# A chunked-attention and gated-MLP kernel: the first weight block is queued behind two inputs, and the second unit's scores and softmax are written ahead of the first unit's values

## The chip, the cores and the metric

The kernel runs on one core of one Trainium2 chip. The metric is the device time of one execution in microseconds. The five engines run side by side, each taking its own instructions in order: TensorE (PE: matmuls and transposes), VectorE (DVE), ScalarE (ACT), GpSimd (POOL) and SyncE (SP, which here issues nearly all transfers). They wait for each other through semaphores.

## The reference

What must be computed, cut to its core (the inputs q and k are drawn with a standard deviation of about 0.4, v with 0.1):

```python
# q, k, v: (8, 8, 576, 64); attention inside chunks of 64 tokens
scores = q_c @ k_c.T / 8;  scores -= max(scores)
attn = exp(scores);  attn /= sum(attn) + 1e-9
out = attn @ v_c
x = out, heads side by side             # (4608, 512)
xn = x / sqrt(mean(x*x) + 1e-6) * rms_g
g = xn @ w_gate                         # (512, 1536)
result = (g * sigmoid(g) * (xn @ w_val)) @ w_out
```

## The kernel before, in words

The 4608 tokens are cut into 18 units of 256 tokens. A unit has two subtiles of 128 tokens, numbered through, so unit 0 is subtiles 0 and 1, and unit 1 is subtiles 2 and 3. The MLP works on tiles of 512 tokens, two units each, and its 1536 hidden columns go in twelve blocks f of 128. The first three MLP tiles are processed one at a time, the rest in pairs. This case is about the stretch before the first MLP matmul and the first two blocks f of the first tile.

**Numbers in two parts.** The matmuls of the MLP run in a rounded 32-bit type, so every operand is split into a high part and a remainder, and each product is three matmuls (high by high, high by low, low by high). A weight block therefore has to be converted before it is used. `conv_load(n)` loads block n (1 MB, tile `raw`) on SP's queue. `conv_start(n)` makes two ACT passes over it (L178, an absolute value into tile `w`, and L179, in place). `conv_join(n)` has three DVE passes (L187, L188, L191) and an ACT cast that writes the high part (L204), and for the gate and value blocks also stores `w` to DRAM. `conv_end(n)` is a DVE subtraction that writes the low part (L212). Block 0 and block 1 are the gate and value weights of f = 0 and f = 1; block 2 is the output weights of both. I call them weights 0, 1 and 2.

**The start of the program** (the plain list of calls from L1091 on):

- `load_first_unit` loads q and k of unit 0 in two halves into the space of `x`, q on SP's queue and k on ACT's. `load_first_values` loads v of unit 0 (512 KB), `load_unit(1)` q, k and v of unit 1 (`qt`, `kt`, `vt`, 512 KB each).
- For each subtile: `scores` (32 small matmuls, L266), `softmax` (DVE maximum and subtraction, ACT exponential L283; for unit 1 both subtiles at once in `softmax_both`, L566, L568, L572), `att_transpose` (4 PE transposes of the exponentials, L324, copied out by ACT, L325), `softmax_sum` (DVE), `att_values` (32 small matmuls with v, L446), and `first_norm` (DVE, L532, which writes `x`).
- Then the RMS norm of a unit: `first_squares` (ACT, L544, which writes its unneeded squares into the subtile's old exponential tile `e`), `first_root` (ACT L145 and a power on POOL, L146), `first_scale` (ACT, L552 and L556, in place on `x`).
- Then `x` is turned by PE (`x_turn_unit`, L506), and written as high parts by ACT (L512, tile `xh`) and low parts by DVE (L518, tile `xl`). With these the first MLP matmuls start (L587). Their two results `ps_g` and `ps_v` lie in the two buffers of one pool; a silu on ACT (L605) reads `ps_g` and sets that buffer free for the next block f.

The tile pool for `e` has two buffers, so the exponentials of subtile 2 go where those of subtile 0 were, and must wait until `first_squares` has used that space.

**What sets the order.** A scheduler places the instructions of each engine, going by its own estimates of time, from the calls in program order; what results is one fixed list for each engine. Only PE's order from the second MLP tile on is held to program order, and all engines' in the down-projection of the pairs. SP's queue is such a list too, and a transfer waits there until the one eight places before it has landed.

Of the kernel before, what the change touches and what calls it, by code (L numbers as in the profile page):

```python
# [80 lines left out]
def tile_chunk_attn_swiglu(  # L81
# [47 lines left out]
    def bank(pool, name):  # L129
        return pool.tile([P, 512], F32, tag=pool_tag[id(pool)], name=name)  # L130
# [36 lines left out]
    def conv_load(n):  # L167
        if n < len(pairs):
            kind, f = pairs[n]
            nc.sync.dma_start(raws[n], w_up[f] if kind == "up" else w_out[f // 2])  # L170
# [56 lines left out]

    state = {}

    def load_unit(u):  # L230
        qt = io.tile([P, NPAIR, UT], F32, tag="io", name="qt")
        kt = io.tile([P, NPAIR, UT], F32, tag="io", name="kt")
        vt = io.tile([P, NPAIR, UT // CH, D], F32, tag="io", name="vt")
        nc.sync.dma_start(qt, qT[u])
        nc.sync.dma_start(kt, kT[u])
        nc.sync.dma_start(vt, v[u])
        for s in range(2):
            state[2 * u + s] = {"q": qt, "k": kt, "v": vt}

    def load_first_unit():  # L240

        qt, kt = (x[:, 2 * i : 2 * i + 2].rearrange("p s (a t) -> p (s a) t", t=UT) for i in range(2))
        for s in range(2):
            part = slice(s * P, (s + 1) * P)
            nc.sync.dma_start(qt[:, :, part], qT[0][:, :, part])
            nc.scalar.dma_start(kt[:, :, part], kT[0][:, :, part])
            state[s] = {"q": qt, "k": kt}

    def load_first_values():
        vt = io.tile([P, NPAIR, UT // CH, D], F32, tag="io", name="vt")  # L250
        nc.sync.dma_start(vt, v[0])
        for s in range(2):
            state[s]["v"] = vt

    def two_banks(pool, name):
        return [bank(pool, f"{name}{j}").rearrange("p (s c) -> p s c", s=2) for j in range(2)]

    def scores(i, banks):
        st, s = state[i], i % 2
        st["s"] = [b[:, s].rearrange("p (a k) -> p a k", k=CH) for b in banks]  # L260
        for pr in range(NPAIR):
            for j in range(2):
                for c in range(2):
                    tok = s * P + c * CH
                    rows = slice(j * D, (j + 1) * D)
                    nc.tensor.matmul(  # L266
                        st["s"][j][c * CH : (c + 1) * CH, pr],
                        st["q"][rows, pr, tok : tok + CH],
                        st["k"][rows, pr, tok : tok + CH],
                        start=True,  # L270
                        stop=True,
                    )
# [12 lines left out]
    def softmax_sum(i):  # L285
        st = state[i]
        rs = st["rs"] = small.tile([P, NPAIR, 2, 1], F32, name="rs")
        nc.vector.tensor_reduce(rs, st["e"], axis=AX.X, op=ALU.add)
        nc.vector.tensor_scalar_add(rs, rs, 1e-9)
        nc.vector.reciprocal(rs, rs)  # L290
# [27 lines left out]
    def att_transpose(i, pool=None):  # L318
        st = state[i]
        e = st["e"].rearrange("p a j k -> p a (j k)")  # L320
        eT = st["eT"] = att.tile([P, NPAIR, P], F32, tag="eT", name="eT")
        pt = bank(pool or ps_a, "ps_t").rearrange("p (a k) -> p a k", k=P)
        for pr in range(NPAIR):
            nc.tensor.transpose(pt[:, pr], e[:, pr], ident)  # L324
        nc.scalar.copy(eT, pt)  # L325
# [112 lines left out]
    def att_values(i, banks):  # L438
        st, s = state[i], i % 2
        eT, vt = st["eT"], st["v"]  # L440
        st["o"] = [b[:, s].rearrange("p (a d) -> p a d", d=D) for b in banks]
        for pr in range(NPAIR):
            for j in range(2):
                for c in range(2):
                    rows = slice(j * CH, (j + 1) * CH)
                    nc.tensor.matmul(  # L446
                        st["o"][j][c * CH : (c + 1) * CH, pr, :],
                        eT[rows, pr, c * CH : (c + 1) * CH],
                        vt[rows, pr, 2 * s + c, :],
                        start=True,  # L450
                        stop=True,
                    )
# [74 lines left out]
    def first_norm(i):  # L527
        st = state[i]
        xs = x[:, i]
        xv = xs.rearrange("p (j b a d) -> p j a b d", j=2, b=2, d=Q)  # L530
        for j in range(2):
            nc.vector.tensor_tensor(  # L532
                xv[:, j],
                st["o"][j].rearrange("p a (b d) -> p a b d", b=2),
                st["rs"][:, :, j].rearrange("p a (o i) -> p a o i", i=1).broadcast_to([P, NPAIR, 2, Q]),
                op=ALU.mult,
            )

    def first_squares(u):
        ss = state["ss", u] = small.tile([P, 2], F32, name="ss_u")  # L540
        for s in range(2):
            st = state.pop(2 * u + s)
            spent = st["e"].rearrange("p a j k -> p (a j k)")
            nc.scalar.activation(spent, x[:, 2 * u + s], AF.Square, accum_out=ss[:, s : s + 1])  # L544
# [13 lines left out]
    def softmax_both(u, banks):  # L558
        both = [state[2 * u + s] for s in range(2)]
        es = [att.tile([P, NPAIR, 2, CH], F32, name="e") for _ in both]  # L560
        mx = small.tile([P, 2, 2, NPAIR, 1], F32, name="mx_u")
        for st, e in zip(both, es):
            st["e"] = e
        for j in range(2):
            by_row = banks[j].rearrange("p s (a k) -> p s a k", k=CH)
            nc.vector.tensor_reduce(mx[:, j], by_row, axis=AX.X, op=ALU.max)  # L566
            for s, (st, e) in enumerate(zip(both, es)):
                nc.vector.tensor_tensor(  # L568
                    e[:, :, j], st["s"][j], mx[:, j, s].broadcast_to([P, NPAIR, CH]), op=ALU.subtract
                )  # L570
        for e in es:
            nc.scalar.activation(e, e, AF.Exp, scale=SCALE)  # L572
# [465 lines left out]
    def unit_steps(u, x):  # L1038
# [26 lines left out]
        def sixth():  # L1065
            for i in both:
                turned_scale(i)

        return [
            lambda: load_unit(u),  # L1070
            first,
            second,
# [16 lines left out]
            self.n += 1  # L1089

    load_first_unit()  # L1091
    conv_load(0)
    load_first_values()
    load_unit(1)
    nc.sync.dma_start(g_col, rms_g)
    for n in range(1, AHEAD):
        conv_load(n)
    s0, s1, s2 = (two_banks(p, "ps_s") for p in (ps_a, ps_h, ps_acc))
# [5 lines left out]
    softmax_sum(0)  # L1104
    att_transpose(1)
    softmax_sum(1)
    o = two_banks(ps_h, "ps_o")
    att_values(0, o)
    first_norm(0)
    o = two_banks(ps_acc, "ps_o")  # L1110
    att_values(1, o)
    first_norm(1)
    scores(2, s2)
    scores(3, s2)
    softmax_both(1, s2)
    first_squares(0)
    first_root(0)
    first_scale(0, False)
# [24 lines left out]
    for t in range(PLAIN):  # L1143
# [39 lines left out]
        for f in range(NF):  # L1183
            g = gated(f, CONVS[f % 2], conv_step)
            if t == 0:
                if f in (0, 5):
                    u = 2 + (f == 5)
                    load_unit(u)
                    sc = two_banks(ps_a, "ps_s")
                    for i in (2 * u, 2 * u + 1):  # L1190
                        scores(i, sc)
                    if f:
                        softmax_rows(u, sc)
                    else:
                        softmax_whole(u, sc)
                elif f in (2, 7):
                    for i in (2 * u, 2 * u + 1):
                        att_transpose(i)
                elif f in (3, 8):
                    o = two_banks(ps_a, "ps_o")  # L1200
                    for i in (2 * u, 2 * u + 1):
                        att_values(i, o)
                    norm_unit(u, o)
                if f == NF - 1:
                    x_transpose((0, 1))
            elif t == 1 and f == NF - 1:
                for dt in range(NDT):
                    x_split(dt, blocks(x)[:, :, dt], slice(0, TT))
# [18 lines left out]
    for b in range(NB):  # L1227
# [3 lines left out]
        if b + 1 < NB:  # L1231
            u = 2 * t + 4
# [82 lines left out]
```

## Time and profile before

| | |
|---|---|
| median of 3 runs | 905.02 us (904.91 to 908.19) |
| the profiled execution | 905.95 us, its span 904.2 us |
| PE busy in the span | 881.3 us (97%) |
| DVE, ACT, POOL busy | 610.7, 482.1, 191.7 us |
| first MLP matmul (L587) starts | 31.23 us |
| granted TensorE clock | 1.00 throughout |

The span is the time between the first and the last recorded instruction; 1.75 us of the profiled execution lie around it. All stage times in this document are microseconds from the start of the span. In a row of the timeline the first number is the start, the second the duration; a bracket at its end tells how long the engine was idle before it, and what ended that. In a row of transfers the last number is the time from issue to landing.

### The profile page before, as it was taken

What the parts mean: (1) busy time and instruction counts of PE and PEld (TensorE: products, weight loads), DVE (VectorE), ACT (ScalarE), POOL (GpSimd) and SP (SyncE); (2) the same over time, 40 slices, a digit from 0 to 9 for tenths busy, and PEclk for the clock granted to TensorE, in tenths of its full rate; (3) what the DMA queues carried; (4) which work ended last, traced back from release to release, by engine and by line L of the source; (5) the groups of instructions that cost most, each with busy time, mean ns of one, the idle gap of its engine ahead of it and who ended that gap; (6) DMA issues with size and microseconds to landing.
All of it is one profiled execution on the core that took longest, in us unless ns stands there. A gap on an engine that the chain in (4) does not pass through costs nothing. (4 is left out here: it accounts for less than half of the span.)

```text
span 904.2 us, 17484 instructions
## 1 busy us (share of the span) xinstructions
PE 881.3 (97%) x6828; PEld 721.2 (80%) x6828; DVE 610.7 (68%) x984; ACT 482.1 (53%) x795; POOL 191.7 (21%) x163
## 2 busy tenths in 40 slices
PE   4899999999999999999999999999999999999998
PEld 3688888888888888887888878887878788888886
DVE  6999865464567755885577997645768953334776
ACT  5998934353457665565556644545647522222452
POOL 0004040342200000233323012332330114323201
PEclk9999999999999999999999999999999999999999
DMA  9799999787987864698887777776876784445342
GB/s 350 280 336 337 329 333 344 247 259 234 296 267 217 260 201 168 256 292 290 308 264 296 316 258 256 273 264 203 302 246 240 275 340 185 158 149 207 165 163 94
DMA packets 85795, 231.85 MB, mean 256 GB/s; under 512 B 8912, under 2 KB 45264, under 8 KB 71504
## 3 DMA queue, kind: packets, MB, share of 16 engines
q1 hardware_dynamic: 84656, 230.20, 72.7%
q8 instruction: 54, 0.88, 0.4%
q10 hardware_dynamic: 1056, 0.52, 0.2%
q14 instruction: 29, 0.24, 0.1%
HBM read 167.25 MB, written 63.44 MB: 255 GB/s over the span
## 5 line engine op out<-in xcount | busy, mean ns | idle before, releaser
L815 PE MATMUL ps_c<-xp,wr 128*128 128x512 f32 x432 | 104.6, 391 | 0.0
L815 PE MATMUL ps_b<-xp,wr 128*128 128x512 f32 x432 | 104.5, 391 | 0.0
L815 PE MATMUL ps_a<-xp,wr 128*128 128x512 f32 x432 | 104.3, 390 | 0.0
L587 PE MATMUL ps_g<-xh,parts 128*128 128x512 f32 x288 | 96.7, 396 | 0.9 <-ACT xh L512 0.6
L587 PE MATMUL ps_v<-xh,parts 128*128 128x512 f32 x288 | 94.9, 390 | 0.0
L815 PEld LDWEIGHTS ps_a<-xp,wr 128*128 128x128 f32 x432 | 80.9, 188 | 17.3 <-DMA wr<-wsd 0.3
L815 PEld LDWEIGHTS ps_b<-xp,wr 128*128 128x128 f32 x432 | 80.7, 188 | 17.0
L815 PEld LDWEIGHTS ps_c<-xp,wr 128*128 128x128 f32 x432 | 80.6, 188 | 17.0
L622 PE MATMUL acc<-parts,gh 128*128 128x512 f32 x288 | 90.0, 394 | 0.0
L587 PEld LDWEIGHTS ps_g<-xh,parts 128*128 128x128 f32 x288 | 54.5, 189 | 13.5 <-ACT xh L512 1.0
L935 ACT CAST gh<-g 128x512 fp32r<-128x512 f32 x72 | 43.6, 621 | 37.3 <-PE ps_c L1024 13.2
L587 PEld LDWEIGHTS ps_v<-xh,parts 128*128 128x128 f32 x288 | 54.2, 188 | 11.2
L903 POOL TENSOR_TENSOR g<-u,u 128x512 f32<-128x512 f32 x18 | 23.2, 1288 | 186.9 <-ACT u L871 70.6
L622 PEld LDWEIGHTS acc<-parts,gh 128*128 128x128 f32 x288 | 53.2, 188 | 11.2
L940 DVE TENSOR_TENSOR gl<-g,gh 128x512 fp32r<-128x512 f32 x72 | 49.3, 695 | 13.1 <-PE ps_c L1024 4.0
L587 PE MATMUL ps_g<-xl,parts 128*128 128x512 f32 x144 | 56.6, 393 | 0.0
L609 DVE TENSOR_TENSOR sg<-ps_v,sg 128x512 f32<-128x512 f32 x36 | 24.7, 686 | 47.0 <-PE ps_v L587 30.4
L622 PE MATMUL acc<-parts,gl 128*128 128x512 f32 x144 | 56.2, 391 | 0.0
L587 PE MATMUL ps_v<-xl,parts 128*128 128x512 f32 x144 | 56.0, 389 | 0.0
L893 POOL TENSOR_TENSOR p<-p,p 128x512 f32<-128x512 f32 x36 | 46.7, 1310 | 33.5 <-DVE p L892 31.8
L815 PE MATMUL ps_d<-xp,wr 128*128 128x512 f32 x216 | 52.3, 391 | 0.0
L871 ACT ACTIVATE p<-p 128x512 f32<-128x512 f32 x36 | 22.6, 632 | 54.4 <-POOL p L893 52.0
(150 smaller groups left out, 1747.4 us busy)
## 6 DMA issues: line engine op xcount, KB each, us to landing
wr<-wsd SPq DMA_DIRECT2D x63, 1024.0 KB, 7.3
wo<-osd SPq DMA_DIRECT2D x30, 1024.0 KB, 7.9
raw<-w_up_dram SPq DMA_DIRECT2D x12, 1024.0 KB, 10.5
vt<-v_dram SPq DMA_DIRECT2D x18, 512.0 KB, 5.3
wsd<-parts SPq DMA_DIRECT2D x18, 512.0 KB, 8.3
qt<-qT_dram SPq DMA_DIRECT2D x17, 512.0 KB, 5.6
kt<-kT_dram SPq DMA_DIRECT2D x17, 512.0 KB, 6.3
away_e<-e SPq DMA_DIRECT2D x28, 256.0 KB, 3.0
```

Of the source, the lines that this page charges most:

```text
L587: nc.tensor.matmul(ps, a[f][:, cols], b[dt], start=(dt == 0 and i == 0), stop=(dt == NDT - 1 and i == 2),)
L609: nc.vector.tensor_tensor(sg, pv, sg, op=ALU.mult)
L622: nc.tensor.matmul(acc[s], a[:, cols], b, start=(f == 0 and i == 0), stop=(f == NF - 1 and i == 2),)
L815: nc.tensor.matmul(ps, w[:, a, m, cols], xp[:, b, kt], start=start and kt == 0 and i == 0, stop=stop and kt == 1 and i == 2, skip_group_ch ...
L871: nc.scalar.activation(t, t if src is None else src, AF.Silu)
L893: nc.gpsimd.tensor_tensor(kp["p5"], kp["p1"], kp["p5"], op=add)
L903: nc.gpsimd.tensor_tensor(g[:, 0, 1], kp["u2"], kept[0]["u2"], op=mult)
L935: nc.scalar.copy(gh, src)
L940: nc.vector.tensor_tensor(gl, src, pair[0].bitcast(F32), op=ALU.subtract)
```

## The change

Two things are written in another order; no instruction is added or removed.

1. The load of weights 0 leaves its place right behind q and k of unit 0, and is issued behind v of unit 0 and q and k of unit 1, ahead of v of unit 1.
2. `scores(2)`, `scores(3)` and `softmax_both(1)` are called ahead of `att_values` and `first_norm` of unit 0.

```diff
-    def load_unit(u):
+    def load_unit(u, then=None):
         ...
         nc.sync.dma_start(qt, qT[u])
         nc.sync.dma_start(kt, kT[u])
+        if then is not None:
+            then()
         nc.sync.dma_start(vt, v[u])
@@
     load_first_unit()
-    conv_load(0)
     load_first_values()
-    load_unit(1)
+    load_unit(1, lambda: conv_load(0))
@@
     softmax_sum(1)
+    scores(2, s2)
+    scores(3, s2)
+    softmax_both(1, s2)
     o = two_banks(ps_h, "ps_o")
     att_values(0, o)
     first_norm(0)
     o = two_banks(ps_acc, "ps_o")
     att_values(1, o)
     first_norm(1)
-    scores(2, s2)
-    scores(3, s2)
-    softmax_both(1, s2)
```

The lists of the engines differ in more places than that, since the scheduler works from the new order. PE's list is the same again from the early part of the second MLP tile on. Lines of the changed kernel have numbers that are higher by 2. Three places matter.

**First, PE, from the transposes of subtile 0 to the values of unit 0** (`ps_t` takes the transposes, `ps_o` the values, `ps_s` the scores, `kt,qt` are k and q of unit 1). Before:

```order
L324 MATMUL ps_t<-ident,e 128x128 x8
L446 MATMUL ps_o_263<-vt,eT 64x64 x2
...
L446 MATMUL ps_o_284<-vt,eT 64x64 x2
L266 MATMUL ps_s_193<-kt,qt 64x64 x2
...
L266 MATMUL ps_s_194<-kt,qt 64x64 x2
L324 MATMUL ps_t<-ident,e 128x128 x8
```

Now:

```order
L326 MATMUL ps_t<-ident,e 128x128 x4
L268 MATMUL ps_s_193<-kt,qt 64x64
L326 MATMUL ps_t<-ident,e 128x128 x4
L268 MATMUL ps_s_193<-kt,qt 64x64
L268 MATMUL ps_s_194<-kt,qt 64x64 x2
...
L448 MATMUL ps_o_306<-vt,eT 64x64 x2
...
L326 MATMUL ps_t<-ident,e 128x128 x4
```

All 64 score matmuls of unit 1 now stand ahead of the 64 value matmuls of unit 0, and the first of them stands ahead of the transposes of subtile 1.

**Second, DVE and ACT, from the softmax of unit 0 to that of unit 1** (`mx_u` and `e` are the maxima and exponentials of unit 1, `w` and `raw` a weight block in conversion). DVE before:

```order
L187 TENSOR_SCALAR w<-w 128x1024
L532 TENSOR_TENSOR x<-ps_o_263,rs 128x4x2x32
...
L188 SCALAR_TENSOR_TENSOR w<-w,raw 128x1024
L532 TENSOR_TENSOR x<-ps_o_283,rs 128x4x2x32
...
L191 SCALAR_TENSOR_TENSOR w<-raw,w 128x1024
L566 TENSOR_REDUCE mx_u<-ps_s_193 128x8
```

DVE now:

```order
L568 TENSOR_REDUCE mx_u<-ps_s_193 128x8
L568 TENSOR_REDUCE mx_u<-ps_s_194 128x8
L534 TENSOR_TENSOR x<-ps_o_306,rs 128x4x2x32
...
L187 TENSOR_SCALAR w<-w 128x1024
L534 TENSOR_TENSOR x<-ps_o_326,rs 128x4x2x32
...
L570 TENSOR_TENSOR e<-ps_s_193,mx_u 128x4x64
L570 TENSOR_TENSOR e<-ps_s_194,mx_u 128x4x64
L188 SCALAR_TENSOR_TENSOR w<-w,raw 128x1024
```

ACT now, in the same stretch:

```order
L327 COPY eT<-ps_t 128x512 x2
L178 ACTIVATE w<-raw 128x1024
L179 ACTIVATE raw<-raw 128x1024
L546 ACTIVATE e,ss_u<-x 128x512 x2
L145 ACTIVATE ss_u<-ss_u 128x2
L574 ACTIVATE e<-e 128x512
L554 ACTIVATE x<-x,ri_u 128x512
L558 ACTIVATE x<-x,ri_u 128x512
L327 COPY eT<-ps_t 128x512
L574 ACTIVATE e<-e 128x512
L178 ACTIVATE w<-raw 128x1024
L327 COPY eT<-ps_t 128x512
```

On DVE the maxima of unit 1 moved ahead of both norms of unit 0, and the last pass over weights 0 (L191) behind the exponentials' subtraction. On ACT the two exponentials of unit 1 are now apart, each ahead of the first pass over weights 1 (before, both stood right behind it); the two passes over weights 0 still stand ahead of the squares of unit 0.

**Third, ACT, from the high parts of `x` of unit 1 to the first silu.** Before:

```order
L512 ACTIVATE xh_121<-ps_x,g_col 128x256
L512 ACTIVATE xh_122<-ps_x,g_col 128x256
L179 ACTIVATE raw<-raw 128x1024
L204 CAST parts<-w 128x1024
L178 ACTIVATE w<-raw 128x1024
L605 ACT_TABLE_LOAD
L605 ACTIVATE sg<-ps_g 128x512
```

Now, from a little earlier on:

```order
L558 ACTIVATE x<-x,ri_u 128x512
L204 CAST parts<-w 128x1024
L514 ACTIVATE xh_119<-ps_x,g_col 128x256
...
L514 ACTIVATE xh_122<-ps_x,g_col 128x256
L204 CAST parts<-w 128x1024
L178 ACTIVATE w<-raw 128x1024
L179 ACTIVATE raw<-raw 128x1024 x2
L607 ACT_TABLE_LOAD
L607 ACTIVATE sg<-ps_g 128x512
```

The cast of weights 0 (the first L204 here) moved from well ahead of the norm of unit 1 to right behind it, and between the last high part and the table load there is now one pass over a weight block more than before.

## The prediction

> **What bounds the kernel now.** I read the stages first (windows: stretch, then busy time and instruction count of PE, its weight loads, DVE, ACT, POOL, then granted clock, DMA share, GB/s), then PE's waits.
>
> ```profile
> 0.00:31.00 31.00, 15.94 (x284) 12.71 (x284) 21.64 (x47) 20.14 (x35) 2.13 (x9) 1.00 0.95 368
> 31.00:140.00 109.00, 108.43 (x721) 89.21 (x722) 93.32 (x120) 85.18 (x135) 21.45 (x10) 1.00 0.90 318
> 140.00:240.00 100.00, 100.00 (x800) 82.25 (x800) 49.66 (x86) 42.47 (x74) 29.46 (x24) 1.00 0.85 270
> ```
>
> From 31 us on PE has no idle time worth naming: 0.57 us in 109, then none in 100. Only the first 31 us, where it idles for 15.06, can give anything. The waits of PE there (total, times, longest):
>
> ```profile
> PE ps_s L266 <- DMA x<-qT_dram: 5.7, 2, 5.1
> PE ps_t L324 <- ACT e L572: 4.5, 1, 4.5
> PE ps_x L506 <- ACT x L552: 2.2, 1, 2.2
> PE ps_g L587 <- ACT sg L605: 0.3, 1, 0.3
> ```
>
> The 5.7 us is the first load and isn't touched. The 4.5 us is unit 1's transposes waiting for its exponentials; the change is at that place. The timeline around it, rows picked and put by engine:
>
> ```profile
> 6.81 1.13 PE L266 MATMUL ps_s<-x 64*64 64x64 f32 x32 [0.59 <-DMA x<-qT_dram]
> 10.10 1.12 PE L324 MATMUL ps_t<-ident,e 128*128 128x128 f32 x4 [0.60 <-ACT e L283]
> 11.60 1.98 PE L446 MATMUL ps_o<-vt,eT 64*64 64x64 f32 x64 [0.39 <-ACT eT L325]
> 13.88 1.98 PE L266 MATMUL ps_s<-kt,qt 64*64 64x64 f32 x64 [0.29 <-DMA kt<-kT_dram]
> 20.39 1.97 PE L324 MATMUL ps_t<-ident,e 128*128 128x128 f32 x8 [4.53 <-ACT e L572]
> 11.12 0.69 DVE L187 TENSOR_SCALAR w<-w 128x1024 f32<-128x1024 f32 x1
> 13.44 1.22 DVE L188 SCALAR_TENSOR_TENSOR w<-w,raw 128x1024 int32<-128x1024 int32 x1
> 14.57 0.75 DVE L532 TENSOR_TENSOR x<-ps_o,rs 128x256 f32<-128x256 f32 x2
> 16.37 1.28 DVE L566 TENSOR_REDUCE mx_u<-ps_s 128x8 f32<-128x512 f32 x2
> 17.57 1.41 DVE L568 TENSOR_TENSOR e<-ps_s,mx_u 128x256 f32<-128x256 f32 x4
> 9.95 1.13 ACT L178 ACTIVATE w<-raw 128x1024 f32<-128x1024 f32 x1
> 11.93 1.15 ACT L179 ACTIVATE raw<-raw 128x1024 int32<-128x1024 uint32 x1
> 15.41 0.63 ACT L544 ACTIVATE e<-x 128x512 f32<-128x512 f32 x1 [1.09 <-DVE x L532]
> 16.52 0.71 POOL L146 TENSOR_TENSOR ri_u<-ss_u,mhalf 128x2 f32<-128x2 f32 x1 [15.23 <-ACT ss_u L145]
> 17.89 0.70 ACT L556 ACTIVATE x<-x,ri_u 128x512 f32<-128x512 f32 x1
> 18.70 1.12 ACT L178 ACTIVATE w<-raw 128x1024 f32<-128x1024 f32 x1
> 19.72 1.14 ACT L572 ACTIVATE e<-e 128x512 f32<-128x512 f32 x2
> ```
>
> Unit 1's scores end at 15.86, yet its exponentials start only at 19.72. Its subtraction (17.57) needs the maxima and unit 0's squares (which use the old buffer of `e`); the exponentials then stood behind the scaling of unit 0 and L178 on weights 1. So the 4.5 us is ACT's and DVE's queue, not late scores.
>
> **The change part by part.** First the transfers (of each its issue in the timeline, then its row in the view of transfers):
>
> ```profile
> 2.35 0.62 SPq L170 DMA_DIRECT2D raw<-w_up_dram  x1
> raw<-w_up_dram SPq DMA_DIRECT2D x1, 1024.0 KB, 7.5
> 3.97 0.43 SPq L235 DMA_DIRECT2D kt<-kT_dram  x1
> kt<-kT_dram SPq DMA_DIRECT2D x1, 512.0 KB, 9.8
> ```
>
> Weights 0 landed at 9.85, `kt` at 13.77. Behind the weights came three blocks of 512 KB (v of unit 0, `qt`, `kt`) in 3.92 us, 1.31 each; the first transfers end at 6.81, where PE's wait ends. Moved ahead of the weights, `kt` lands at 6.81 + 3.92 = 10.73 at the earliest. The 1 MB of weights 0 took 3.04 after 6.81 where two blocks at 1.31 take 2.62, so 0.42 of start-up may be added: 11.15. I take 10.9. **Weights 0 land at 13.8**, in `kt`'s old place, since the same bytes are ahead of them: 3.9 later. No transfer is added, and the ones behind land as before; the weights hold up no later load.
>
> PE. The first score matmul of unit 1 stands ahead of subtile 1's transposes and waits for `kt`: the transposes start at 11.0 (before 10.10), end at 12.0; the 64 scores (1.98) end at 14.0, 1.9 earlier than before; the 64 value matmuls (1.98) end at 16.0, 2.4 later.
>
> DVE. It has nothing to do until the scores end: maxima 14.0 + 1.3 = 15.3, first norm (0.7 to 0.75 a subtile) 16.0, L187 on weights 0 (0.69; its ACT pass ended at 13.8 + 1.1 = 14.9) 16.6, second norm 17.3 where it was 15.32. This is the price of moving the values back: +2.0 on unit 0's norm.
>
> ACT (whose next instruction overlaps the one before by about 0.1: 18.70 + 1.12 is past the next start, 19.72, by that). L178 and L179 on weights 0 fill 13.8 to 16.0. The squares of subtile 1 follow the second norm and end with their read-out at 18.1, the small scale at 18.3; the first exponential of unit 1 (0.63) stands next, **18.3 instead of 19.72**; POOL's power (0.71) ends at 19.0; the two scalings, which ended at 18.59, end at 20.4. Then the copy of subtile 2's transposes (0.6), the second exponential (ends 21.4), L178 on weights 1 (1.04 until the next can start), and the copy of subtile 3 (PE's transposes took 1.1 and end at 22.5) at 22.6. That was at 23.31: 0.7 is left of the 1.4 gained. The rest of the way, rows picked from the timeline:
>
> ```profile
> 23.31 0.59 ACT L325 COPY eT<-ps_t 128x512 f32<-128x512 f32 x1
> 23.78 1.07 ACT L204 CAST parts<-w 128x1024 fp32r<-128x1024 f32 x1
> 26.99 0.47 ACT L512 ACTIVATE xh<-ps_x,g_col 128x256 fp32r<-128x256 f32 x1
> 27.35 0.21 ACT L145 ACTIVATE ss_u<-ss_u 128x2 f32<-128x2 f32 x1
> 29.00 0.71 ACT L556 ACTIVATE x<-x,ri_u 128x512 f32<-128x512 f32 x1
> 31.23 0.80 PE L587 MATMUL ps_g<-xh,parts 128*128 128x512 f32 x1 [0.56 <-ACT xh L512]
> 37.30 1.28 ACT L605 ACT_TABLE_LOAD   x1
> 38.52 0.39 PE L587 MATMUL ps_v<-xh,parts 128*128 128x512 f32 x1
> 38.60 0.60 ACT L605 ACTIVATE sg<-ps_g 128x512 f32<-128x512 f32 x1
> 39.25 0.50 PE L587 MATMUL ps_g<-xh,parts 128*128 128x512 f32 x1 [0.34 <-ACT sg L605]
> 44.82 0.61 PE L622 MATMUL acc<-parts,gh 128*128 128x512 f32 x2
> 47.63 1.16 PE L266 MATMUL ps_s<-kt,qt 64*64 64x64 f32 x64
> ```
>
> From 22.6 on ACT is the queue that matters: copy (0.5), L179 on weights 1 (1.05), two high parts of unit 0 (0.9), L178 on weights 2 (1.05) bring it to 26.5. Two squares (1.2), a high part, the small scale at 28.1 (before 27.35); then POOL's 0.71 and the scalings, done at 30.4 (before 29.71): +0.7. L191 on weights 0, which DVE now does only near 20 to 21.5, lets the cast (L204) come late; ACT has it right here, 30.4 to 31.4. Only then come unit 1's first two high parts, and **the first MLP matmul at 32.3, +1.1**. But the four transposes that stood behind the first two matmuls are done by then, so the 24 matmuls of f = 0 end where they ended: the last starts near 38.5.
>
> The first silu is next. After the last high part at 34.15 ACT has L204 (0.95), L178 (1.04), two L179 (1.06 each) and the table load (1.28): the silu starts at 39.5 where it was 38.60, ends at 40.1, and frees `ps_g` for f = 1, which starts at 40.1 and not 39.25: **+0.9**. From there PE is the bound again if the weights keep ahead. DVE is then behind by an L187 and an L188 (0.69 + 1.22) and by the 0.9 itself, but the low part of the output weights of f = 0 is written by 43.1 in this walk, and PE asks for them 5.57 after f = 1 starts (44.82 - 39.25), at 45.7. I add nothing; with that cover gone, it would cost what is missing of these 2.6.
>
> Sum: 0.9 on the profiled 905.95, or 906.8; that execution lay 0.93 above the median of 905.02, so the prediction for the median is **905.9 us**. Bounds: were ACT never to wait from 13.8 on, its work up to the silu (23.1 us: the rows of its list from L178 on weights 0 to the table load, by these durations) would end at 36.9, 1.7 ahead of before; and the landing's +-0.3 and ACT's small waits give +-1.3 on the other side.
>
> [...] The granted clock reads 1.00 everywhere, but the same 64 score matmuls took 1.98 us at 13.88 and 1.16 at 47.63, so the trace agrees with two rates. [...] I keep the sum at the slow durations.
>
> **The rivals.** *A: the earlier exponential carries through.* For it: 4.53 is the longest wait after the first load, and the exponential does move forward by 1.4. If ACT's waits closed up on the way (1.7 above), PE would start f = 1 about 1.5 earlier: 903.5. The whole 4.53 would give 900.5. Against it: unit 0's norm, 2.0 later, feeds the scalings on the same engine. *B, the slower side: the late weights at the head of ACT's queue.* L178 on weights 0 waits for its transfer ahead of the squares; what stands behind is late once that pass starts after 14.6, for its two passes and the first squares (2.1 + 0.6) then run past 17.3, where the second norm ends. If the 3.92 passed down the list whole, 905.0 + 3.9 = 908.9. For it: both engines go in order, and DVE's L187 stands ahead of the second norm. Against it: until 16.0 DVE has no norm ready either, so most of the 3.9 lies under the scores and maxima of unit 1. *C: nothing moves at the end*: the high parts run a little earlier, the silu's delay is taken up in front of f = 1, and it is 905.0.
>
> **How the numbers follow.** My forecast 0.62 (its own range 904.6 to 907.2), A 0.18 (0.03 of it for the whole gap), B 0.10, C 0.10. The range goes down to 903.3, which takes in most of A and the gap-free ACT, and up to 908.0, which leaves out the heart of B: about 0.82. A measurement of this kernel can tell about 0.5%, 4.5 us, from no change. Faster than 900.5 is only A whole, 0.03; slower than 909.5 is B with something on top, 0.04; 0.93 is left for the same.
>
> **What would show it.** Unit 1's scores ending near 14, the values near 16; L178 on weights 0 starting at 13.8; unit 1's first exponential near 18.3; the wait of its transposes down from 4.5 to about 2.9; the last scaling near 30.4; the first MLP matmul near 32.3, and f = 1 near 40.1 behind a wait for the silu of about 1 us. PE idling anywhere later, for weights, would break the step where I added nothing; a first MLP matmul ahead of 31 would be A, one behind 34 B.

## The result, and the profile after

The changed kernel takes 913.55 us (median of 6 runs, 912.45 to 914.91), the kernel before 905.4 beside it (904.69 to 908.19): a ratio of 1.0075, 95% interval 1.0059 to 1.009. It is **slower by about 7 us** (6.8 by the ratio; the two medians lie 8.2 apart) where 905.9 was forecast and 908.0 was the upper end of the range. The profiled execution took 912.45 us with a span of 910.7; before it was 905.95 and 904.2. The stages of the changed kernel (columns as in the prediction):

```profile
0.00:31.00 31.00, 14.79 (x280) 11.77 (x280) 18.29 (x44) 17.27 (x31) 2.65 (x9) 0.81 0.86 322
31.00:140.00 109.00, 104.42 (x688) 84.30 (x689) 92.69 (x116) 87.67 (x135) 21.14 (x10) 0.98 0.89 313
140.00:240.00 100.00, 100.00 (x808) 82.46 (x807) 51.62 (x88) 43.92 (x75) 26.36 (x23) 1.00 0.83 271
```

The clock of 0.81 in the first stage isn't itself a loss: the reading falls to 0.50 from about 19 to 36 us, but the first MLP matmul takes 0.80 us there, as it did in the kernel before at a reading of 1.00.

PE is as full as before from 140 us on. But between 31 and 140 it has 4.6 us of idle time where it had 0.6. PE's waits in the changed kernel:

```profile
PE ps_t L326 <- ACT e L574: 3.6, 1, 3.6
PE ps_x L508 <- ACT x L554: 3.1, 1, 3.1
PE ps_t L326 <- ACT e L308: 2.6, 1, 2.6
PE ps_s L268 <- DMA kt<-kT_dram: 1.7, 1, 1.7
PE ps_g L589 <- ACT sg L607: 1.5, 2, 1.0
PE ps_o L448 <- ACT eT L327: 1.5, 1, 1.5
```

Four rows are of the start, and the row of `ps_g` is so in part: 1.0 of it is the wait of f = 1, 0.51 a wait at 96.19. The third is new and lies elsewhere: L308 is the exponential of `softmax_rows`, the softmax of unit 3, a hundred microseconds into the program. To see where the time went I paired the MLP matmuls (L587 before) of two kernels by rank and subtracted their starts. The "lag" of the changed kernel, at these times of the kernel before:

| before, us | 31.2 | 39.6 | 75.6 | 93.2 | 104.1 | 111.7 | 298.0 |
|---|---|---|---|---|---|---|---|
| lag, us | +2.20 | +2.27 | +2.32 | +2.99 | +6.05 | +6.55 | +6.56 |

So there are **two losses: 2.3 us at the start, and 4.2 between 85 and 112 us**. At the end of the span 6.5 is left of both.

**The start.** Rows of the changed kernel's timeline, picked and put by engine:

```profile
7.78 1.13 PE L268 MATMUL ps_s<-x 64*64 64x64 f32 x32 [1.54 <-DMA x<-qT_dram]
11.61 0.44 PE L268 MATMUL ps_s<-kt,qt 64*64 64x64 f32 x2 [1.65 <-DMA kt<-kT_dram]
14.70 1.55 PE L448 MATMUL ps_o<-vt,eT 64*64 64x64 f32 x63
33.42 0.80 PE L589 MATMUL ps_g<-xh,parts 128*128 128x512 f32 x1
41.52 0.50 PE L589 MATMUL ps_g<-xh,parts 128*128 128x512 f32 x1 [1.00 <-ACT sg L607]
17.49 0.75 DVE L534 TENSOR_TENSOR x<-ps_o,rs 128x256 f32<-128x256 f32 x2
18.82 1.22 DVE L188 SCALAR_TENSOR_TENSOR w<-w,raw 128x1024 int32<-128x1024 int32 x1
19.95 0.75 DVE L570 TENSOR_TENSOR e<-ps_s,mx_u 128x256 f32<-128x256 f32 x2
19.44 1.16 POOL L146 TENSOR_TENSOR ri_u<-ss_u,mhalf 128x2 f32<-128x2 f32 x1 [18.15 <-ACT ss_u L145]
13.98 1.14 ACT L178 ACTIVATE w<-raw 128x1024 f32<-128x1024 f32 x1 [0.27 <-DMA raw<-w_up_dram]
19.20 0.61 ACT L574 ACTIVATE e<-e 128x512 f32<-128x512 f32 x1
21.26 0.70 ACT L558 ACTIVATE x<-x,ri_u 128x512 f32<-128x512 f32 x1
31.19 0.71 ACT L558 ACTIVATE x<-x,ri_u 128x512 f32<-128x512 f32 x1
40.87 0.60 ACT L607 ACTIVATE sg<-ps_g 128x512 f32<-128x512 f32 x1
```

The second half of unit 0's q arrived at 7.78 in this execution and not at 6.81. That comes and goes: 6.81 and 7.02 in two of the runs below with the same start, 7.58 in one with the start of before. The lag at f = 1 of the first two is +2.05 and +2.09, so it isn't the cause.

**Unit 3.** ACT's timeline in the kernel before, the ends of the pieces:

```profile
87.35 1.28 ACT L306 ACT_TABLE_LOAD   x1 [0.44 <-DVE mx_u L301]
88.65 0.31 ACT L306 ACTIVATE e<-ps_s,mx_u 128x64 f32<-128x64 f32 x1
...
91.25 0.60 ACT L605 ACTIVATE sg<-ps_g 128x512 f32<-128x512 f32 x1
91.87 1.28 ACT L306 ACT_TABLE_LOAD   x1
...
98.30 1.28 ACT L605 ACT_TABLE_LOAD   x1
99.59 0.60 ACT L605 ACTIVATE sg<-ps_g 128x512 f32<-128x512 f32 x1
```

and in the changed kernel:

```profile
92.53 1.28 ACT L308 ACT_TABLE_LOAD   x1 [0.75 <-DVE mx_u L303]
93.82 0.31 ACT L308 ACTIVATE e<-ps_s,mx_u 128x64 f32<-128x64 f32 x1
94.25 1.28 ACT L607 ACT_TABLE_LOAD   x1
95.54 0.60 ACT L607 ACTIVATE sg<-ps_g 128x512 f32<-128x512 f32 x1
96.15 1.28 ACT L308 ACT_TABLE_LOAD   x1
...
102.23 1.28 ACT L607 ACT_TABLE_LOAD   x1
103.52 0.60 ACT L607 ACTIVATE sg<-ps_g 128x512 f32<-128x512 f32 x1
104.14 1.28 ACT L308 ACT_TABLE_LOAD   x1
105.43 0.31 ACT L308 ACTIVATE e<-ps_s,mx_u 128x64 f32<-128x64 f32 x1
```

In these rows each change between exponential and silu brings a table load of 1.28 us on ACT. Before, the sixteen exponentials stood in two pieces, 4 | 12, all ahead of the second silu shown (the eighth of the program). Now they stand as 1 | 14 | 1: one piece more, and the last exponential alone behind that silu and two table loads. PE needs all sixteen for its transposes:

```profile
96.19 0.50 PE L589 MATMUL ps_g<-xh,parts 128*128 128x512 f32 x1 [0.51 <-ACT sg L607]
101.77 0.60 PE L326 MATMUL ps_t<-ident,e 128*128 128x128 f32 x4
105.89 0.66 PE L326 MATMUL ps_t<-ident,e 128*128 128x128 f32 x4 [2.59 <-ACT e L308]
```

In the kernel before no wait stands at this place. The lists of ACT and DVE are made anew for the whole program from the new order of the calls, so an edit at 10 us can place an exponential at 105 us.

### The profile page after: what moved, and what is told of

It reads as the page before. It is cut to its first block, busy times and chain, and to the rows that moved or that the text cites. A ratio compares the mean times of both kernels' runs of the same rounds, so it can differ in the third digit from the quotient of the medians.

```text
span 910.7 us, 17495 instructions
## 1 busy us (share of the span) xinstructions
PE 882.3 (97%) x6828; PEld 720.7 (79%) x6828; DVE 611.4 (67%) x984; ACT 485.4 (53%) x797; POOL 192.1 (21%) x163
## 4 chain that ended last, share of the span: by engine, by line
PE 85%; DMA 5%; DVE 5%; ACT 3%; issue 1%; SPq 1%; POOL 0%; DVEq 0%; POOLq 0%; ACTq 0%
PE ps_c L817 11%; PE ps_b L817 11%; PE ps_a L817 11%; PE acc L624 9%; PE ps_g L589 8%; PE ps_v L589 8%; PE ps_d L817 5%; PE ps_c L1026 5%; PE ps_a L1026 5%; PE ps_b L1026 5%; PE ps_d L1026 2%; PE ps_o L390 2%; PE ps_s L268 2%; DMA wr<-wsd 2%; DMA kt<-kT_dram 1%
```

## The experiments

Each kernel ran beside the kernel before on its chip; ratios are to that. Line numbers shift by up to 6 with the edits. The theories: **L**, the start's loss is the late weights; **O**, it is the reordering; **S**, unit 3's loss is how the list places exponentials among silus; **B**, unit 3 is late because the start is. P, Q, S2 and W come up later and are told where they are tested.

**The two parts alone.** One kernel has only the calls reordered, one only the load moved.

```diff
 # e1_scores_only: after, without
-    load_unit(1, lambda: conv_load(0))
+    conv_load(0)    # behind load_first_unit, as before
+    load_unit(1)
 # e2_load_only: after, with scores(2), scores(3), softmax_both(1) behind first_norm(1) again
```

> Second half of the change alone: scores and softmax of unit 1 ahead of unit 0's values, the load of weights 0 in its old place. Theory L (the late weights cost the start of the MLP): weights 0 land near 9.9 again, and f = 1 starts within 0.7 us of the kernel before (39.25). Theory O (moving the values behind the scores costs it): f = 1 starts 1.5 us or more late, near 41. Both then see the list of ACT near 90 us: unit 3's sixteen exponentials stand in three pieces (1, 13, 2) with silus between. Theory S (the piece behind the second silu stalls PE by about 2.6 to 3.2 us, at the transposes of unit 3): a wait of PE for the exponentials of 2.5 or more, total 909 to 912. Theory B (that wait is only the conversion's backlog on DVE): no such wait where the weights come early, total 905 to 907.

> First half of the change alone: weights 0 loaded behind v of unit 0 and q and k of unit 1, program order of scores and values as before. Theory L: weights 0 land near 13.8, their first ACT pass starts there, f = 1 starts 2 us or more late (41.3). Theory O: f = 1 within 0.7 us of 39.25. The exponentials of unit 3 are in three pieces here too (1, 11, 4): theory S: a wait of 2.6 to 3.5 at unit 3's transposes, so 910 to 913 with L's delay and 908 to 910 with O's; theory B: the wait is there only with L's delay.

Reordering alone: 910.51 (ratio 1.0046, 1.0028 to 1.0063), a lag of +1.2 at f = 1 and +3.65 at 104 us. Load alone: 911.55 (1.0054, 1.0033 to 1.0074), -0.16 at f = 1, then +3.54 at 104 and +4.14 at 112. L falls: late weights alone cost the start nothing. The reordering costs it 1.2, less than O's 1.5, and 2.1 to 2.4 with the late load under it. And B is in trouble, for the load's kernel isn't late at 85 us, yet loses 4.3 there. Its exponentials ran as 1 | 11 | 4, those of the other as 1 | 12 | 3 (not 13 and 2). S's sizes missed too: PE's waits for the last piece were 1.73 in the load's kernel and 2.08 in the other, shorter than S allowed, and the load's 911.55 lies above S's 910 (beside a kernel before at 907.18 here). The load's kernel waits another 0.93 for the silu behind the first piece.

**The last piece brought forward, and its control.** Unit 3's exponentials get a higher priority, in the changed kernel and in the one before.

```diff
+            with tc.high_priority(offset=250):
                 for j in range(2):
                     for pr in range(NPAIR):
                         nc.scalar.activation(e[:, pr, j], ...)   # softmax_rows
```

> The changed kernel with a higher priority for unit 3's exponentials: ACT's list is the changed kernel's up to there, then all exponentials stand ahead of the second silu (pieces of 1 and 15 and no third one behind it). Theory S (the one exponential behind a silu and two table loads is the 2.6 us wait, and with it the loss of 4.2 us from 93 to 108 us): the wait falls under 0.6, the lag behind the kernel before stays at +2.3 to +3.2 past 110 us, total about 910 (913.5 less 3.5). Theory B (DVE's maxima, 5.2 us late, are what is late, however the exponentials are cut): PE waits as long at another place there, total 912.5 to 914.5.

> Control: the same priority on the kernel before, whose exponentials already stand in two pieces (4 and 12) ahead of the second silu and stay so. Both theories: 905.4 +- 1, no wait of PE at unit 3's transposes.

The changed kernel now has 1 | 15 and takes 910.1 (1.0035, 1.0023 to 1.0048); the lag is +2.05 at f = 1 and +3.92 at 112 us, 2.6 less than without. In the kernel before the list stays 4 | 12, and the time 906.65 (0.9998, 0.9984 to 1.0011). Between 85 and 112 us 1.8 were still lost, more than S allowed (a lag of at most +3.2): PE waits 0.51 for the silu behind the first piece, 0.22 for the last exponentials and 0.23 for a weight block's low part, and the first matmuls behind such a wait start 0.34 us apart for 0.23.

**All sixteen in one piece, ahead of a silu.** The offset is 300.

> The changed kernel with the sixteen exponentials of unit 3 marked urgent, so that they stand in ScalarE's list in one piece behind five silus: two table loads there instead of five, nothing left behind a later silu. Theory S (the way the list cuts the exponentials costs the second half of the loss): PE's lag behind the kernel before is +2.0 to +2.3 us at f=1 and still at most +2.5 at 112 us; the time is 2 to 2.5 us above the kernel before. Rival B (the work is late because the start is late): the lag grows to about +4 by 112 us, as in the run with two pieces, and the time is 3.5 to 4.5 us above.

914.81 (1.0087, 1.007 to 1.0103): S's numbers missed, and B's too. The piece now stands ahead of the seventh silu of the program (the text above counts one too few), and pulls PE's transposes forward with it. That silu starts at 100.03, behind 4.7 us of exponentials and two table loads; PE waits three times:

```profile
96.70 1.22 PE L327 MATMUL ps_t<-ident,e 128*128 128x128 f32 x4 [0.92 <-ACT e L309]
98.77 1.11 PE L327 MATMUL ps_t<-ident,e 128*128 128x128 f32 x4 [0.86 <-ACT e L309]
100.68 0.79 PE L590 MATMUL ps_g<-xh,parts 128*128 128x512 f32 x1 [0.79 <-ACT sg L608]
```

By the third, PE's granted clock is down as well (0.50 in this stage):

```profile
100.00:104.00 4.00, 3.32 (x8) 2.64 (x9) 3.10 (x4) 3.99 (x6) 0.00 (x0) 0.50 0.93 255
```

Of the 6.6 us lost there, 2.6 are these three waits; about 2 are ten MLP matmuls at the lower clock, 0.43 from start to start where 0.23 is usual. So few table loads aren't enough: what counts is what stands ahead of the silu, or of the transpose, that PE reaches next. This became theory S2.

**The same cut put into the kernel before.** Its start is untouched; the last exponential gets a lower priority, which gives 4 | 11 | 1.

```diff
+                    with order_of(s * 2 * NPAIR + j * NPAIR + pr):   # 15: offset -90
                         nc.scalar.activation(e[:, pr, j], ...)
```

> The kernel before with the last of unit 3's sixteen exponentials given a lower priority, so that they stand in three pieces, 4 | 11 | 1, the last alone behind one more silu and two more table loads; the start is untouched. Theory S: no lag until 90 us, then PE waits 1.5 to 2.6 us on that exponential and the lag stays: 2 to 4 us slower than before. Rival B: without a late start the cut is covered by the MLP's matmuls, and the time is within 0.5 us of before.

911.5 (1.0048, 1.003 to 1.0066). The lag is +0.27 at 93 us, +4.83 at 104, +5.34 at 112. **This cut costs the old kernel 5 us**, with no change at the start; S had allowed at most 4. B falls: a late start isn't needed. The wait, and the stages behind it:

```profile
105.22 0.66 PE L330 MATMUL ps_t<-ident,e 128*128 128x128 f32 x4 [3.02 <-ACT e L312]
...
108.89 1.05 PE L593 MATMUL ps_g<-xh,parts 128*128 128x512 f32 x2
```

```profile
104.00:108.00 4.00, 2.79 (x11) 2.32 (x12) 3.38 (x7) 3.99 (x7) 0.00 (x0) 0.81 1.04 393
108.00:112.00 4.00, 4.00 (x15) 3.19 (x14) 3.30 (x3) 3.97 (x6) 0.00 (x0) 0.76 0.95 337
```

The wait is 3.0, more than the 2.6 allowed for; the rest goes with slower matmuls behind it (below). It isn't the price of one moved exponential alone, for the list moved more. Behind the fifteenth stand not only a silu and two table loads but also three passes over weight blocks:

```profile
98.45 1.10 ACT L209 CAST parts<-w 128x1024 fp32r<-128x1024 f32 x1
99.39 1.21 ACT L183 ACTIVATE w<-raw 128x1024 f32<-128x1024 f32 x1
...
102.41 1.04 ACT L209 CAST parts<-w 128x1024 fp32r<-128x1024 f32 x1
...
104.76 0.31 ACT L312 ACTIVATE e<-ps_s,mx_u 128x64 f32<-128x64 f32 x1
```

They take 3.2 us of ACT. PE began to wait at 102.2, so by my estimate from these rows the exponential would have come about in time without them. In the changed kernel nothing but the silu and the loads stands there, and PE waits 2.59.

**One piece behind the seventh silu** (called the sixth in the texts below, too). The scaling of the maxima gets a lower priority (offset -60), the exponentials a higher one (280): in the changed kernel, and in the one with the load's move alone.

> The changed kernel with unit 3's sixteen exponentials in one piece, as in the run with urgent exponentials, but behind the sixth silu and not ahead of it (the maxima's scaling gets a lower priority, the exponentials a higher one); the start is as changed. Theory S2 (what costs is a table load or exponential that stands ahead of a silu or a transpose that TensorE reaches, wherever the start ends): lag +2.0 to +2.3 us at f=1 and at most +2.7 at 112 us; the time is 2.0 to 2.8 us above the kernel before. Rival B (the softmax of unit 3 is late because the start is late): the lag still grows to +4 or more by 112 us.

> The move of the load alone, with the same placing of unit 3's sixteen exponentials behind the sixth silu. Theory S2: no lag at f=1 (-0.3 to +0.3), at most +0.5 at 112 us, and a time within 0.7 us of the kernel before, where the load's move with its three pieces was 4.4 us above. Rival W (the later weights of step 0 make the vector and scalar engines late for all that follows, and that costs at unit 3): the lag still grows by 2 us or more between 85 and 112 us.

The changed kernel: 909.14 (1.003, 1.0019 to 1.0042), a lag of +2.09 at f = 1, +2.12 at 93, +2.88 at 112, just past S2's bound. The load alone: 908.12 (1.0011, 1.0 to 1.0022), +0.43 at f = 1 (S2 had at most +0.3), then +1.83: 1.3 us above the kernel before, more than S2's 0.7. The 1.4 that it loses at unit 3 lie between S2 (a lag of at most +0.5) and rival W (2 or more), so neither is borne out there. ACT's rows in the first of the two:

```profile
92.89 0.58 ACT L609 ACTIVATE sg<-ps_g 128x512 f32<-128x512 f32 x1
...
95.82 0.31 ACT L310 ACTIVATE e<-ps_s,mx_u 128x64 f32<-128x64 f32 x1
...
100.46 0.71 ACT L614 CAST gh<-sg 128x512 fp32r<-128x512 f32 x1
101.19 1.28 ACT L609 ACT_TABLE_LOAD   x1
```

The exponentials start at 95.82, 7.2 us later than before, and PE's transposes wait for none of them. Here the late softmax holds up no transpose, and with the same late start the cut list cost 4.2: its place among the silus decides. Of the loss at unit 3, 0.8 is left here: PE waits 0.45 for a low part of the gated values, whose cast (L614) stands behind the whole piece.

**A tile of its own for unit 0's exponentials.** `e` of unit 0 comes from another pool, so unit 1's exponentials needn't wait for the squares that use it; in the changed kernel, the one before, and the one with the calls reordered alone.

```diff
-        e = st["e"] = att.tile([P, NPAIR, 2, CH], F32, name="e")
+        e = st["e"] = tmp_tile("e").rearrange("p (a j k) -> p a j k", j=2, k=CH)
```

> The changed kernel with unit 0's exponential tile taken from the pool of work tiles, so that unit 1's exponentials need not wait for a tile that the squares of unit 0's norm write; the list then has them straight behind the scores, and unit 3's sixteen in one piece. Theory P (the shared tile held unit 1's exponentials back to 19 us): the first of unit 1's begins at 15 to 16 us, PE's lag at f=1 is 0 or below (-1 to +0.5), and the time is 0 to 1.5 us below the kernel before. Rival Q (the start is set by unit 0's scalings and by GpSimd's power, whenever unit 1's exponentials come): the lag at f=1 stays +1.5 to +2.3 and the time is about 2 us above.

> The kernel before with the same other tile for unit 0's exponentials and nothing else; its exponentials of unit 3 stay 4 | 12. A control: all theories expect the time within 0.5 us of before, and the lag within 0.3 us at f=1.

> The reordered scores and softmax alone, with weights 0 ahead as before, and unit 0's exponentials in a tile of their own; unit 3's sixteen then stand in one piece between two silus. Theory P (the shared tile is 1.4 us of the start's loss): the lag at f=1 is -0.3 to +0.2 where the reordering alone had +1.2, nothing is lost at unit 3, and the time is 0 to 0.7 us below the kernel before. Rival Q: the lag at f=1 is +1 and the time 1 us above.

Changed: 907.39 (1.0007, 0.9996 to 1.0019), +0.78 at f = 1, +1.92 at 112. Before: 906.85 (1.0002, 0.9989 to 1.0014). Reordered alone: 906.43 (0.9994, 0.9983 to 1.0005), -0.50 at f = 1, +0.26 at 112. The lists of the first and the third have unit 3's sixteen in one piece behind the seventh silu, and lose nothing there, although the first is 1.9 late; 1.1 and 0.8 go elsewhere, between 40 and 76 us. The tile takes 1.5 to 1.7 off the start in both: P's size of 1.4 was right, its landing point in the changed kernel (at most +0.5, and a time below the kernel before, which is 0.9 above) not quite. In that kernel unit 1's first exponential ran at 17.69, not by 16, behind DVE's subtraction. So no version beats the kernel before; the two best can't be told from it.

## Why the prediction was wrong, point by point

| step | predicted | measured |
|---|---|---|
| `kt` there | 10.9 (to 11.15) | 11.61; 11.20 to 11.95 in the other runs with this start |
| weights 0 there | 13.8 | 13.98 |
| unit 1's scores end | 14.0 | 15.00 |
| unit 0's values end | 16.0 | 16.25 |
| second norm ends | 17.3 | 18.24 |
| first exponential of unit 1 | 18.3 | 19.20 |
| power on POOL ends | 19.0 | 20.60 |
| scalings of unit 0 end | 20.4 | 21.96 |
| last scaling ends | 30.4 | 31.90 |
| first MLP matmul | 32.3 | 33.42 |
| last matmul of f = 0 starts | 38.5 | 40.13 |
| silu starts | 39.5 | 40.87 |
| f = 1 starts | 40.1, +0.9 | 41.52, +2.27 |
| after f = 1 | nothing | +4.2 |

**The step that failed is "I add nothing".** It asked only whether the weights keep ahead of PE. They did: in the changed kernel no wait for weights stands between 40 and 112 us. What broke was ACT's order at unit 3, where the change shows nothing in the calls. The places compared all lay ahead of f = 1; ACT's list past them had already changed from 4 | 12 to 1 | 14 | 1, and the prediction didn't price it. Its own sign, PE idling anywhere later, came true, though for exponentials and not for weights.

**The start had the right mechanism and was too small by 1.4.** All steps come in the predicted order, and the silu wait of about 1 us is there (1.00). Of the difference, 0.7 enters with `kt`, which arrived past the upper bound (0.5 in the runs where it came at 11.35 and 11.40), and 0.3 behind it: two score matmuls ran ahead of subtile 1's transposes, which started 0.4 after `kt` where the walk had 0.1. Another 0.5 enters at POOL: the power, taken at 0.71 from the kernel before, took 1.16. These pass down ACT's queue nearly whole, as the walk had it: its last scaling is 1.5 late, the silu 1.4. That the late weights cost nothing alone (-0.16) fits the reading that most of their delay lies under other work.

The walk kept PE's slow durations and was a little long with them: 63 value matmuls took 1.55 us where 64 had taken 1.98. The gain ended behind ACT's queue and isn't seen at f = 1. The first transposes of unit 1 came 3.62 us of idle PE later, and four took 1.12, as slow as before.

Rival A (the gain carries through) fails on the norm of unit 0, as argued against it. Rival B (late weights at the head of ACT's queue) had a slower side, but its sign, a first MLP matmul behind 34, didn't come, and the load alone left the start as it was. Rival C fails with the start.

**What stays open**: why the scheduler cuts the exponentials as it does; and why the load's move still loses 1.4 us between 97 and 107 us with one piece. By the starts of PE's matmuls 0.4 of it lies in the transposes, whose second half waits for the last exponentials (0.10 shown), 0.3 in the output matmuls, where no wait is shown, and 0.6 at a weight block's low part (0.32 shown). Whether the later weights delay that low part wasn't tried. I didn't take the late `kt` and the longer power away by themselves.

## What to carry to other kernels

Where a scheduler makes the lists, compare every engine's list over the whole program, not only around the edit, and look where functions that each need a table load alternate (exponential and silu here, 1.28 us a load): count the loads, and find what stands alone behind a silu that PE will ask for. An average of 53% busy on ACT says nothing there. Exponentials that were 7 us late held up no transpose here, while a list that left the last one behind a silu, two table loads and three weight passes cost 5.

## What was not expected of the hardware

**Behind a wait of 3.02 us the matmuls were slow, behind one of 2.59 they weren't.** With the exponential put last in the old kernel, PE stood still for 3.02 us, and two matmuls then took 1.05 us where they take 0.62: granted clock 0.81 and 0.76 in the two stages shown. From 106.40 to 110.05 nine matmuls took 3.65 us where 0.23 from start to start gives 2.07; by this estimate 1.6 of the loss of 5 us are slow matmuls, beside the 3.0 of wait. In the changed kernel the wait was 2.59, the granted clock read 1.00, and the matmuls behind it ran as before. But the longest wait alone doesn't decide it: in the run with all sixteen in one piece ahead of a silu it was 0.92, and the granted clock still fell to 0.50 from about 99 to 105.5 us. There PE had run only eight transposes between 95.8 and 100.7. What brings the clock down, these runs don't show.

**POOL's power was longer beside a DVE pass over weights.** Its 1.16 us in the changed kernel ends at 20.60, 0.65 after DVE's L188 gave way to the next instruction at 19.95. With the tile of its own it took 1.73:

```profile
21.28 1.73 POOL L146 TENSOR_TENSOR ri_u<-ss_u,mhalf 128x2 f32<-128x2 f32 x1 [19.99 <-ACT ss_u L145]
21.23 1.22 DVE L188 SCALAR_TENSOR_TENSOR w<-w,raw 128x1024 int32<-128x1024 int32 x1
22.36 0.20 DVE L292 RECIPROCAL rs<-rs 128x8 f32<-128x8 f32 x1
```

Again it ends (23.01) 0.65 after L188 gives way, and ACT's scalings waited behind it. With the calls reordered alone the second power took 1.05, beside L187, and ended at 29.53, 0.65 after L187 gave way at 28.88. That POOL waits there for DVE's pass to end is my reading of these three rows. In the kernel before, where DVE was reading scores at that moment (L566), the power took 0.71. No run took the overlap away from the changed kernel.
